# Two heads on the partition halves for the attention scores of a block-sparse attention and cos-MLP kernel on Trainium2

## The chip, the core and the metric

The kernel runs on one core of one Trainium2 chip. The metric is the time of one execution on the device in microseconds (us), as the median of several runs. The core has five engines that work side by side, each through its own list of instructions in a fixed order: TensorE (PE in the profile: matmuls; its weight loads stand apart as PEld), VectorE (DVE), ScalarE (ACT), GpSimd (POOL) and SyncE (SP), which here issues nearly all DMA transfers and does nothing else. Engines wait for each other by semaphores. TensorE and the others share no queue, but an instruction that waits holds back all that stand behind it in its own engine's list.

## What is computed

```python
def _attn_ref(q, k, v, sampled_blocks):           # 4 batches, 8 heads, 768 rows, 64 columns, fp32
    scores = np.matmul(q, k.transpose(0, 1, 3, 2)) / np.sqrt(D)
    mask = np.abs(blk_i - blk_j) <= 1              # blocks of 32 rows: 24 of them
    mask = mask | (blk_i == 0) | (blk_j == 0) | (blk_i == n_blocks - 1) | (blk_j == n_blocks - 1)
    for qb in range(n_blocks):
        for kb in sampled_blocks[qb]:              # three random blocks of keys for each block of queries
            mask[qb * block:(qb + 1) * block, kb * block:(kb + 1) * block] = True
    scores = np.where(mask, scores, -1000000000.0)
    attn = softmax(scores)
    return np.matmul(attn, v)

def _moe_ref(x, w_in, w_out):                      # x: 3072 x 512, w_in: 512 x 2048, w_out: 2048 x 512
    h = x @ w_in
    return (h * np.cos(h)) @ w_out
```

The output of the attention, laid out as 3072 rows of 512, is the x of the second function. All inputs are fp32.

## The kernel before

**Numbers.** Every fp32 operand of a matmul is split into two fp16 parts, a scaled high part and a low part (what the high part leaves). A product then takes several fp16 matmuls that add up in one PSUM bank: for the values and the MLP the terms high·high, high·low and low·high, for the scores all four.

**Tiles.** Queries are taken in 24 tiles of 128 rows, six for each batch. Five of them are sparse: each of a tile's four query blocks sees 11 blocks of keys, which are 352 columns, 256 of them common to the tile and 96 gathered for the block. The sixth is dense: the first and last block of the batch, which see all 768 keys, and the last 64 rows between. A unit of a sparse tile is a pair of heads (four units), one of a dense tile is one head (eight units). Two tiles make one step of the MLP, 256 rows (12 steps).

**A unit of attention.** `sparse_scores` (L1519) or `dense_scores` (L1545) write the scores of two heads, or of one head's two halves of keys, into the two banks of `sp`, of which there is one. `add_max` (L1558) adds the mask bias on VectorE, writes the result to `P` (four buffers) and keeps the row's maximum; `neg_max` (L1574) makes the bias of the exponent, `exp` (L1582) runs on ScalarE, `p_hi` and `p_lo` split the result into `ring` (three buffers), `p_transpose` (L1613) has a DMA transpose it into `PT` (three buffers), and `sparse_values` or `dense_values` multiply it with `V` into `xp`. `normalize` and `x_transpose` (L1678) turn a finished tile into its half of `xT`, from which `feed_forward` reads (L1828 up, L1878 down, which are matmuls of 256 and of 512 columns).

**The scores before.** Keys lie in `W` with the high part of one head in rows 0 to 63 and its low part in rows 64 to 127. Queries lie in `U` (two buffers) in two copies, one with high over low and one with low over high. Each copy times `W` is a matmul with all 128 rows, which makes two of the four terms at once. In a sparse unit each head and copy has one matmul of 192 columns (L1530), one of 64 (L1531), and four small ones of 96 columns (L1536) whose outputs are 32 rows each, which lie beside each other on the array (`tile_position=(0, 32 * j)`). This is `sparse_scores`:

```python
for z in range(2):
    u = U[:, z, h, :]
    mm(spv[:, :, 0:96], u, keys[:, :, 64 * i : 64 * i + 96], start=(z == 0), stop=False)
    mm(spv[:, :, 96:128]..., u, ends, start=False, stop=False)
```

**The copies of the queries.** For a tile after the fourth, `u_transpose` (L1457) has a DMA transpose the split queries from the buffer `n` into the first copy, and `u_swap` (L1462, L1464) has two more DMAs of 64 rows, which wait for the first, write the second copy from it. For the first four tiles `u_flip` (L1472, L1476) does both with TensorE, in two rounds with an eviction each by `u_put` (L1376, the shared `copy`).

**What sets the order.** `plan_kernel` (L522) makes all steps of all engines with an engine, a cost in us and a position; the position is a nominal one plus offsets from two tables, `PARAMS` and, by name, `NUDGES`. `Plan.run` (L397) then runs a list schedule over them: it takes the step that can start first by a simple model of the costs and, among those close to it, the one with the lowest position. It also hands out buffers, in the order of positions. The result is one fixed list for each engine; on the chip every engine follows its list and waits where the model was wrong.

Of the kernel before, what the change touches and what calls it, by code (L numbers as in the profile page):

```python
# [11 lines left out]
BF16 = mybir.dt.bfloat16  # L12
# [8 lines left out]
P = 128  # L21
# [35 lines left out]
NUDGES = dict(  # L57
    idx=-32.59, regs=19.28, regs0=-1.07, regs0_0=-2.88, regs1=6.62, regs1_0=10.29, regs2=1.07, regs2_0=-31.56, regs0_1=12.92, const=-2.31,
    kload=-0.13, kload0=-30.46, kload0_0=-8.81, ksq=11.63, ksq0=-3.65, ksq0_0=-30.09, ksq0_1=-32.78, kload0_2=-49.17, ksq0_2=1.23, kred=16.57,
    kred0=-13.01, kall=1.85, kall0=-40.47, ksc=-3.94, ksc0=-9.83, regs3=24.18, regs3_0=17.71, regs4=10.59, regs4_0=31.84, regs2_1=15.93,  # L60
    regs3_1=4.55, regs4_1=12.48, vload=2.48, vload0=-13.26, vload0_0=22.33, vsq=-5.99, vsq0=10.15, vsq0_0=50.09, vload0_1=0.11, vsq0_1=3.22,
    vload0_2=35.38, vsq0_2=9.63, vred=33.96, vred0=-15.73, vall=-0.58, vall0=2.01, vsc=-8.12, vsc0=2.74, ql=-1.06, ql0=8.22, qsq0=8.45, qsc=-7.13,
    qsc0=-6.37, qu=-1.96, qu0=-0.02, qnu=-18.18, qnu0=-9.18, qhi=-0.93, qhi0=-10.88, qlo=-5.87, qlo0=-9.35, uT=-0.55, uT0=-4.6, up=-0.48, up0=-6.98,
    khi=7.77, khi0=14.43, klo=15.69, klo0=21.95, kT=-0.02, kT0=6.82, kT0_2=1.62, kp=12.59, kp0=-20.67, kp0_2=2.03, kT0_3=0.47, kp0_3=-1.32,
    kT0_4=24.6, kp0_4=0.92, kT0_5=2.53, kp0_5=14.95, vhi=1.54, vhi0=14.31, vhi0_0=-0.32, vlo=5.56, vlo0=-1.09, vlo0_0=16.98, vst=7.46, vst0=36.73,
    vst0_0=3.28, vhi0_1=-5.72, vlo0_1=-16.01, vst0_1=28.16, vhi0_2=-26.22, vlo0_2=-5.63, vst0_2=12.95, vhi0_3=15.2, vlo0_3=0.02, vst0_3=27.76,
    vhi0_4=3.17, vlo0_4=3.32, vst0_4=-20.04, vhi0_5=27.65, vlo0_5=0.16, vst0_5=-21.14, vg=3.73, vg0_0=1.06, vg0_1=8.15, vg0_2=-14.78, vi=-7.5,
    vi0=6.3, vi0_0=-2.36, vi0_1=-12.83, vi0_3=13.91, wgd=-2.2, wgd0=-12.59, wga=0.68, wga0=20.44, wl=-4.41, wl0=-1.67, wc=-1.12, wc0=-0.25,
    wc0_0=0.05, wc0_1=-14.61, wsq=-3.18, wsq0=-2.46, wl1=-0.33, wc1=6.19, wc1_0=0.22, wc1_1=-3.2, wc1_2=3.2, wsq1=5.1, wl2=-26.1, wl3=-3.84,
    wc3_0=-0.59, wc3_1=-0.14, wc3_2=-6.37, wsq3=-2.11, wred=-0.94, wred0=-3.35, wall=1.38, wall0=23.2, wsc=-13.63, wsc0=-2.06, whi=0.24, whi0=13.15,  # L70
    wsi=-0.66, wsi0=-4.4, wlm=2.01, wlm0=-1.65, wlp=0.08, wlp0=-6.52, wlm1=0.71, wlp1=-7.37, whi2=-18.32, wlm2=1.35, wlp2=-0.9, wlm3=0.12,
    wlp3=-0.69, wl4=-7.09, wl5=-6.48, wc5=-5.38, wc5_0=15.11, wc5_1=-21.89, wc5_2=-1.33, wsq5=10, wl6=0.91, wl7=-14.86, wc7_1=25.08, wc7_2=12.48,
    wsq7=-30.63, wred4=17.52, wall4=2.06, wsc4=14.76, whi4=-4.06, wsi4=-2.52, wlm4=-4.15, wlp4=1, wlp5=5.53, whi6=-1.48, wlm6=-11.21, wlp6=6.93,
    wlp7=-6.67, wl8=-12.18, wl9=2.08, wc9=-7.98, wc9_0=-46.39, wc9_1=-4.24, wc9_2=-2.56, wsq9=-16.66, wl10=-1.79, wl11=17.97, wc11=-11.77,
    wc11_0=-2.11, wc11_1=-2.56, wc11_2=8.32, wsq11=-9.29, wsc8=2.64, whi8=32.97, wsi8=1.58, wlp8=-19.15, wlp9=-10.75, whi10=-17.36, wlm10=0.43,
    wlp10=-1.39, wlm11=4.47, wlp11=19.28, wl12=0.19, wl13=-22.97, wc13=14.49, wc13_0=-3.33, wc13_1=1.32, wc13_2=-12.78, wsq13=0.05, wl14=-1.87,
    wc14=-6.2, wc14_0=-7.86, wc14_1=-29.23, wc14_2=-4.96, wl15=31.58, wc15=-1.92, wc15_0=-3.83, wc15_1=20.07, wc15_2=-7.97, wsq15=1.03, wred12=6.05,
    wall12=9.18, wsc12=6.51, whi12=-11.82, wsi12=-6.71, wlm12=-1.47, wlp12=-0.2, wlm13=-2.27, wlp13=-5.13, whi14=-0.55, wlm14=-0.53, wlp14=1.2,
    wlm15=1.5, wlp15=-8.08, wl17=21.8, wc17=0.4, wc17_0=-16.55, wc17_1=-2.31, wc17_2=-2.05, wsq17=9.14, wl18=-1.04, wc18=-13.01, wc18_0=-2.02,
    wc18_1=3.07, wc18_2=-0.49, wsq18=6.03, wl19=-5.87, wc19=-0.16, wc19_0=8.28, wc19_1=-2.96, wc19_2=-5.86, wsq19=5.44, wred16=3.84, wall16=7.65,  # L80
    wsc16=-0.99, wlo=1.65, wlo16=-18.71, whi18=23.86, wlo18=2.49, wl20=3.86, wl21=-31.15, wc21=3.34, wc21_0=-3.38, wc21_1=-8.22, wc21_2=-20.01,
# [1875 lines left out]
```

## Time and profile before

| | |
|---|---|
| median of 3 runs | 894.15 us (890.65 to 894.72) |
| span of the profiled execution | 858.9 us |
| own time of the profiled execution | not recorded apart from its span; median less span is 35.25 us |
| TensorE busy in the span | 745.0 us, 87% |
| VectorE busy | 636.3 us, 74% |
| ScalarE busy | 640.3 us, 75% |

The span runs from the first to the last instruction of the profiled execution; the time of a run also holds what lies around it. Busy times are sums of an engine's instructions, so an engine at 87% was idle or waiting in the other 13%. The profile puts a wait down to what came last. "SPq" is the queue of SyncE, that is, the issue of a transfer; "DMA" is the transfer itself.

### The profile page before, as it was taken

What the parts mean: (1) busy time and instruction counts of PE and PEld (TensorE: products, weight loads), DVE (VectorE), ACT (ScalarE), POOL (GpSimd) and SP (SyncE); (2) the same over time, 40 slices, a digit from 0 to 9 for tenths busy, and PEclk for the clock granted to TensorE, in tenths of its full rate; (3) what the DMA queues carried; (4) which work ended last, traced back from release to release, by engine and by line L of the source; (5) the groups of instructions that cost most, each with busy time, mean ns of one, the idle gap of its engine ahead of it and who ended that gap; (6) DMA issues with size and microseconds to landing.
All of it is one profiled execution on the core that took longest, in us unless ns stands there. A gap on an engine that the chain in (4) does not pass through costs nothing.

```text
span 858.9 us, 23175 instructions
## 1 busy us (share of the span) xinstructions
PE 745.0 (87%) x9320; PEld 513.9 (60%) x9320; DVE 636.3 (74%) x1624; ACT 640.3 (75%) x1220; POOL 98.5 (11%) x128
## 2 busy tenths in 40 slices
PE   2575875888999988989999998999999879999997
PEld 2444563454757646847766557767675558576583
DVE  3987979898877775876857886968769756867361
ACT  1686956998868996896857988688769757869351
POOL 5212110000040012200030030200030112000000
PEclk9975896998999997999999998999999879999999
DMA  9999983669997998998895999896977995955300
GB/s 251 328 234 193 265 255 86 111 161 161 197 233 126 190 183 180 170 183 141 208 206 115 215 209 195 167 197 117 219 166 126 180 208 126 204 88 117 87 1 26
DMA packets 313308, 146.57 MB, mean 171 GB/s; under 512 B 266224, under 2 KB 290928, under 8 KB 313200
## 3 DMA queue, kind: packets, MB, share of 16 engines
q1 hardware_dynamic: 308080, 129.35, 73.4%
q0 software_dynamic: 5120, 15.73, 7.5%
q8 instruction: 73, 1.20, 0.6%
q14 instruction: 35, 0.29, 0.1%
HBM read 68.23 MB, written 12.58 MB: 94 GB/s over the span
## 4 chain that ended last, share of the span: by engine, by line
PE 51%; DMA 19%; DVE 15%; ACT 8%; issue 4%; SPq 2%; POOL 0%; DVEq 0%; ACTq 0%
PE ph L1828 19%; PE po L1878 19%; DMA PT<-ring 8%; DMA stage<-in_k_dram 3%; PE xp L1636 3%; DMA xT<-n 2%; PE sp L1530 2%; PE sp L1547 2%; DVE P L1563 2%; DVE ring L1599 2%; PE xp L1624 2%; PE sp L1536 2%; ACT P L1585 1%; DVE n L1287 1%; DVE g L1869 1%
## 5 line engine op out<-in xcount | busy, mean ns | idle before, releaser
L1828 PE MATMUL ph<-xT,w 128*128 128x256 f16 x2304 | 268.1, 276 | 8.6 <-DMA xT<-n 4.8
L1878 PE MATMUL po<-w,g 128*128 128x512 f16 x1152 | 269.2, 382 | 5.1 <-ACT g L1866 1.5
L1828 PEld LDWEIGHTS <-w 128*128 128x128 f16 x2304 | 225.7, 99 | 45.1 <-issue 4.3
L1878 PEld LDWEIGHTS <-g 128*128 128x128 f16 x1152 | 108.3, 98 | 125.1 <-issue 6.6
L1585 ACT ACTIVATE P<-P,sm 128x352 f32<-128x352 f32 (+1 forms) x224 | 151.9, 680 | 18.6 <-DVE sm L1578 9.4
L1502 POOL DMA_INDIRECT V<-scr,gidx x80 | 85.8, 1073 | 625.9 <-PE xp L1624 317.3
L1599 DVE TENSOR_TENSOR ring<-P,ring 128x704 f16<-128x704 f32 (+1 forms) x112 | 99.5, 906 | 37.1 <-ACT ring L1595 37.1
L1595 ACT CAST ring<-P 128x704 f16<-128x704 f32 (+1 forms) x112 | 86.0, 786 | 14.8 <-DMA PT<-ring 14.5
L1837 ACT ACTIVATE hs<-ph,sm 128x512 f32<-128x512 f32 x96 | 64.0, 679 | 44.0 <-PE ph L1828 39.6
L1563 DVE CUSTOM_DVE_ANT_1 P<-sp,bias 128x352 f32<-128x352 f32 x160 | 78.4, 518 | 23.3 <-PE sp L1536 22.6
L1530 PE MATMUL sp<-W,U 128*128 128x192 f16 x320 | 52.6, 265 | 21.0 <-DVE sm L1563 17.5
L1860 DVE SCALAR_TENSOR_TENSOR hs<-hs,sm,g 128x1024 f32<-128x1024 f32 x48 | 61.2, 1282 | 12.8 <-ACT g L1855 12.3
L1855 ACT ACTIVATE g<-g,sm 128x1024 f32<-128x1024 f32 x48 | 54.8, 1146 | 16.6 <-DVE g L1851 16.1
L1869 DVE TENSOR_TENSOR g<-hs,g 128x1024 f16<-128x1024 f32 x48 | 58.5, 1221 | 10.2 <-ACT g L1866 10.2
L1866 ACT ACTIVATE g<-hs 128x1024 f16<-128x1024 f32 x48 | 50.3, 1050 | 12.2 <-DVE hs L1860 11.9
L1851 DVE SCALAR_TENSOR_TENSOR g<-g,hs 128x1024 f32<-128x1024 f32 x48 | 58.5, 1221 | 0.8
L1847 DVE TENSOR_SCALAR g<-hs 128x1024 f32<-128x1024 f32 x48 | 32.9, 690 | 30.5 <-ACT hs L1837 29.0
L1624 PE MATMUL xp<-V,PT 96*32 96x64 f16 x1920 | 32.0, 205 | 24.0 <-DMA PT<-ring 20.9
L1531 PEld LDWEIGHTS <-U 128*128 128x128 f16 x320 | 33.0, 103 | 25.9 <-issue 22.2
L1531 PE MATMUL sp<-W,U 128*128 128x64 f16 x320 | 48.0, 205 | 0.0
L1636 PE MATMUL xp<-V,PT 128*128 128x64 f16 x960 | 47.2, 204 | 0.0
L1624 PEld LDWEIGHTS <-PT 96*32 96x32 f16 x1920 | 22.0, 103 | 39.7 <-DMA PT<-ring 26.8
(182 smaller groups left out, 939.3 us busy)
## 6 DMA issues: line engine op xcount, KB each, us to landing
V<-scr SPq DMA_DIRECT2D x20, 384.0 KB, 4.1
stage<-in_k_dram SPq DMA_DIRECT2D x12, 512.0 KB, 5.6
w<-in_moe_w_in_dram SPq DMA_DIRECT2D x12, 512.0 KB, 5.8
w<-in_moe_w_out_dram SPq DMA_DIRECT2D x12, 512.0 KB, 4.5
V<-scr SPq DMA_DIRECT2D x8, 768.0 KB, 5.2
scr<-n SPq DMA_DIRECT2D x21, 256.0 KB, 3.4
qs<-in_q_dram SPq DMA_DIRECT2D x20, 256.0 KB, 4.9
U<-U SPq DMA_DIRECT2D x40, 128.0 KB, 2.9
```

What stands on the lines that cost most here:

```text
L1502: self.nc.gpsimd.indirect_dma_start(V[:96, 2 + j, :], None, self.scr[b][:, :], bass.IndirectOffsetOnAxis(ap=self.gidx[:96, c : c + 1], axi ...
L1530: mm(spv[:, :, 0:96], u, keys[:, :, 64 * i : 64 * i + 96], start=(z == 0), stop=False)
L1531: mm(spv[:, :, 96:128].rearrange("p y (n c) -> p y n c", c=hf), u, ends, start=False, stop=False)
L1563: self.nc.vector.tensor_tensor_reduce(out=self.p_view(n, Pt)[:, a].rearrange("p (n c) -> p n c", c=hf), in0=sp[:, :w].rearrange("p (n c) - ...
L1585: self.nc.scalar.activation(Pv[:, a], Pv[:, a], AF.Exp, scale=qc[:, 4:5], bias=nb[:, bcol : bcol + 1], accum_out=sums[:, 2 * j + a : 2 * j ...
L1595: self.nc.scalar.copy(R[:, :, 0, : self.width(n)], self.p_view(n, Pt))
L1599: self.nc.vector.tensor_tensor(R[:, :, 1, :w], self.p_view(n, Pt), R[:, :, 0, :w], ALU.subtract)
L1624: mm(xp[32 * j : 32 * j + 32, h, :], PT[:96, 6 * a + 3 * l + 2, 32 * j : 32 * j + 32], V[:96, 2 + j, h, d0:d1], start=(a == 0 and x == 0), ...
L1636: mm(xp[:, h, :], PT[:, 6 * a + 3 * l + c, :], V[:, c, h, d0:d1], start=False, stop=(a == 1 and c == 1 and x == len(terms) - 1),)
L1828: self.nc.tensor.matmul(ph[:, ff, :], self.W1[p][:, wl, cc, c * P : (c + 1) * P], xT[:, xl * NCC + cc, :], start=(j == 0), stop=(j == len( ...
L1869: self.nc.vector.tensor_tensor(g[:, 1024:2048], hs, g[:, 0:1024], ALU.subtract)
L1878: self.nc.tensor.matmul(po, g[:, gl, ff, t * P : (t + 1) * P], self.W2[p][:, wl, ff, :], start=(first and ff == half * hf and j == 0), sto ...
```

## The change

The two heads of a pair now lie over each other: rows 0 to 63 of `W` hold one head and rows 64 to 127 the other, for the high parts in one place and for the low parts in another (`k_split`, `q_view`). A term of a score is then a matmul with 64 rows for each head, at row 0 or row 64 of the array, and a head has three terms instead of four: low·low is left out. The second copy of the queries is not made: `u_swap` and `u_flip` are gone, `U` is half as large, and the first four tiles use one round of transposes and one eviction.

- A sparse unit goes from 8 large and 16 small matmuls to 12 and 24, each with 64 rows.
- A unit of a dense tile becomes a pair of heads with one half of the keys (still eight units in a tile): 6 matmuls of 384 columns in place of 4. Both halves must be there before `neg_max` and `exp`, so `neg_max` runs once for every two units, for two heads at a time.
- The planner takes the positions of all steps from a new table, `PLACES`, has other costs, and a simple model of DMA (`DMAS`, `DMA_AHEAD`). So the order of all engines is new.

PE's list grows from 18594 to 20514 rows, SP's falls from 403 to 360 (the 40 transfers from `U` to `U` are gone), DVE's falls from 1770 to 1747, and ACT's grows from 923 to 951, with 46 loads of a function table in place of 42.

```diff
-            for z in range(2):
-                u = U[:, z, h, :]
-                mm(spv[:, :, 0:96], u, keys[:, :, 64 * i : 64 * i + 96], start=(z == 0), stop=False)
-                mm(spv[:, :, 96:128].rearrange("p y (n c) -> p y n c", c=hf), u, ends, start=False, stop=False)
...
+    def pairs(self, unit, U, W):
+        f, x = divmod(unit, 2)
+        hi = 4 * f + x
+        for ul, wl in ((0, 0), (0, 1), (1, 0)):
+            yield ul == 0 and wl == 0, ul == 1, U[:, 4 * ul + unit, :], W[:, hi + 2 * wl]
...
+            for part in range(2):
+                for a in range(2):
+                    r = slice(a * D, a * D + D)
...
+                    mm(out, u[r], x, start=(first and not part), stop=False, tile_position=(a * D, 0))
+        for _, final, u, keys in self.pairs(unit, U, Wg):
+            for j in range(4):
+                for a in range(2):
...
+                        tile_position=(a * D, 32 * j),
...
+    def dense_scores(self, unit, c, U, sp2):
...
+                self.nc.tensor.matmul(
+                    sp2[:, a, :384], u[r], keys[r, 384 * c : 384 * c + 384], start=first, stop=final, tile_position=(a * D, 0)
+                )
...
-    def u_swap(self, U, k):
-        D = self.D
-        if k:
-            self.nc.sync.dma_start(U[D : 2 * D, 1], U[0:D, 0])
-        else:
-            self.nc.sync.dma_start(U[0:D, 1], U[D : 2 * D, 0])
...
-            nc.vector.tensor_tensor(mx[:, 2:3], mx[:, 0:1], mx[:, 1:2], ALU.max)
-            nc.vector.tensor_scalar(nb[:, 0:1], mx[:, 2:3], nu, LN_PSCALE, op0=ALU.mult, op1=ALU.add)
...
+            nc.vector.tensor_tensor(mx[:, 0:2], mx[:, 0:2], mx[:, 2:4], ALU.max)
+        nc.vector.tensor_scalar(nb, mx[:, 0:2], nu, LN_PSCALE, op0=ALU.mult, op1=ALU.add)
...
-    idx=-32.59, regs=19.28, regs0=-1.07, regs0_0=-2.88, regs1=6.62, regs1_0=10.29, regs2=1.07, regs2_0=-31.56, regs0_1=12.92, const=-2.31,
...
+        o.pos = self.places.get(name if n == 1 else f"{name}#{n}", pos)
```

Three places show what moves. In the rows a name like `U_95` is one buffer of a tile, and the sizes are partitions by elements.

**SP at the queries of the tenth tile (batch 1).** Before, `U_95` is that tile's buffer; `n_90` are its split queries, `PT` and `ring` belong to the units of the tile ahead of it, `V_106` and `qs_93` to tiles to come.

```order
L1614 DMA_TRANSPOSE PT_104<-ring_100 128x12x128
L1457 DMA_TRANSPOSE U_95<-n_90 128x8x128
L1679 DMA_TRANSPOSE xT_110<-n_91 128x8x128
L1496 DMA V_106<-scr_122 16x2048
L1424 DMA qs_93<-in_q_dram 128x8x64
L1464 DMA U_95<-U_95 64x1024
L1462 DMA U_95<-U_95 64x1024
L1614 DMA_TRANSPOSE PT_103<-ring_100 128x12x128
L1614 DMA_TRANSPOSE PT_105<-ring_101 128x12x128
L1614 DMA_TRANSPOSE PT_104<-ring_102 128x12x128
```

After, `U_94` from `n_91` is the tenth tile's, and `U_94` held the ninth tile's queries too; `U_95` from `n_92` is the eleventh's, issued ahead of it.

```order
L1704 DMA_TRANSPOSE PT_105<-ring_100 128x12x128
L1556 DMA_TRANSPOSE U_95<-n_92 128x8x128
L1771 DMA_TRANSPOSE xT_109<-n_90 128x8x128
L1704 DMA_TRANSPOSE PT_103<-ring_101 128x12x128
L1704 DMA_TRANSPOSE PT_104<-ring_102 128x12x128
L1556 DMA_TRANSPOSE U_94<-n_91 128x8x128
L1704 DMA_TRANSPOSE PT_105<-ring_100 128x12x128
L1704 DMA_TRANSPOSE PT_103<-ring_101 128x12x128
L1704 DMA_TRANSPOSE PT_104<-ring_102 128x12x128
```

The two transfers from `U` to `U` are gone from between the transposes of `ring`. The tenth tile's queries now go into the buffer that the tile before it uses, so that transfer cannot start until that tile's last score. The same holds for the tiles 13, 15, 18 and 21; before, the two buffers alternated from tile to tile but once (at the tile 19).

**DVE at the second unit of a dense tile.** Before, the unit is one head; L1563 is `add_max` with its accumulator row behind it, L1577 and L1578 are `neg_max`, L1599 is `p_lo`.

```order
L1563 ISA P_97,sm<-sp_114,dbias 128x384
L1563 ISA sm 128x1
L1599 TENSOR_TENSOR ring_100<-P_98,ring_100 128x2x384
L1577 TENSOR_TENSOR sm<-sm 128x1
L1578 TENSOR_SCALAR sm<-sm 128x1
L1563 ISA P_98,sm<-sp_114,dbias 128x384
```

After, L1654 is `add_max`, L1668 and L1669 are `neg_max`, L1689 is `p_lo`; `P_97` is the second half of the keys of the first pair of heads, whose first half, `P_96`, stands some 20 rows ahead. The list is shown from the second of the two `add_max` on.

```order
L1654 ISA P_97,sm<-sp_114,dbias 128x384
L1654 ISA sm 128x1
L1755 TENSOR_SCALAR sm<-sm 128x8
L1961 TENSOR_TENSOR g_86<-hs_83,g_86 128x1024
L1762 RECIPROCAL sm<-sm 128x8
L1668 TENSOR_TENSOR sm<-sm 128x2
L1669 TENSOR_SCALAR sm<-sm 128x2
L1986 SCALAR_TENSOR_TENSOR kn_88<-po_119,sm,kn_88 128x512
L1689 TENSOR_TENSOR ring_102<-P_99,ring_102 128x2x352
L1689 TENSOR_TENSOR ring_101<-P_98,ring_101 128x2x352
L1654 ISA P_99,sm<-sp_114,dbias 128x384
```

Before, `neg_max` came once for every head, that is, for every unit; now it comes after every second unit and covers two heads, so that the first half waits in its buffer until the second is there.

**SP at the start of the program.** Before, the first rows are the sampled blocks, three loads of keys, three of values, the first queries and the first weights.

```order
L1144 DMA V_106<-in_sampled_blocks_dram 128x144
L1329 DMA stage_79<-in_k_dram 128x8x128
L1329 DMA stage_80<-in_k_dram 128x8x128
L1329 DMA stage_81<-in_k_dram 128x8x128
L1329 DMA hs_82<-in_v_dram 128x8x128
L1329 DMA hs_83<-in_v_dram 128x8x128
L1329 DMA g_84<-in_v_dram 128x8x128
L1424 DMA qs_93<-in_q_dram 128x8x64
L1714 DMA w_3_71<-in_moe_w_in_dram 128x1024
```

After, a load of output weights stands ahead of the keys.

```order
L1241 DMA V_106<-in_sampled_blocks_dram 128x144
L1806 DMA g_84<-in_moe_w_out_dram 128x1024
L1426 DMA stage_79<-in_k_dram 128x8x128
L1426 DMA stage_80<-in_k_dram 128x8x128
L1426 DMA stage_81<-in_k_dram 128x8x128
L1426 DMA hs_82<-in_v_dram 128x8x128
L1806 DMA w_3_71<-in_moe_w_in_dram 128x1024
L1523 DMA qs_93<-in_q_dram 128x8x64
L1426 DMA hs_83<-in_v_dram 128x8x128
```

The load of 512 KB into `g_84` moved from behind the keys and values to the second place, and one load of input weights moved ahead of the first queries.

## Rows read from the trace of the kernel before

**Rows 1.** The head of the profile's page and its line of busy times.

```profile
span 858.9 us, 23175 instructions
...
PE 745.0 (87%) x9320; PEld 513.9 (60%) x9320; DVE 636.3 (74%) x1624; ACT 640.3 (75%) x1220; POOL 98.5 (11%) x128
```

**Rows 2.** The chain of work that ended last, followed back from the last instruction: shares of the span by engine.

```profile
PE 51%; DMA 19%; DVE 15%; ACT 8%; issue 4%; SPq 2%; POOL 0%; DVEq 0%; ACTq 0%
```

**Rows 3.** Busy time of each engine in two stretches of the span, and in 20 us near the start (the last three columns are the granted clock of TensorE as a part of full speed, the busy share of the DMA engines and GB/s).

```profile
0.00:200.00 200.00, 130.50 (x1792) 90.27 (x1793) 163.12 (x451) 143.64 (x276) 33.05 (x68) 0.85 0.83 207
200.00:859.00 659.00, 614.51 (x7530) 423.67 (x7528) 473.13 (x1174) 496.67 (x945) 65.45 (x60) 0.97 0.81 159
20.00:40.00 20.00, 10.52 (x120) 8.79 (x120) 18.91 (x48) 12.63 (x21) 3.29 (x3) 1.00 1.03 326
```

**Rows 4.** What TensorE waited for between 200 and 859 us (engine, line and what came last; us in total, times, longest us).

```profile
PE xp L1624 <- DMA PT<-ring: 13.6, 10, 3.5
...
PE ph L1828 <- DMA xT<-n: 4.8, 3, 2.2
PE xp L1650 <- DMA PT<-ring: 3.5, 3, 1.4
```

**Rows 5.** The same view for the whole span, the two lines of the scores.

```profile
PE sp L1530 <- DVE sm L1563: 17.5, 14, 3.0
...
PE sp L1547 <- DVE sm L1563: 6.1, 3, 2.7
```

**Rows 6.** The timeline of TensorE at one sparse unit between two rounds of down matmuls (start us, us, operation; the length is that of the record from its start to its modelled end, and neighbours overlap).

```profile
663.16 0.25 PE L1530 MATMUL sp<-W,U 128*128 128x192 f16 x1
663.25 0.19 PE L1531 MATMUL sp<-W,U 128*128 128x64 f16 x1
663.28 0.25 PE L1530 MATMUL sp<-W,U 128*128 128x192 f16 x1
...
663.58 0.19 PE L1531 MATMUL sp<-W,U 128*128 128x64 f16 x1
663.71 0.35 PE L1536 MATMUL sp<-Wg,U 128*32 128x96 f16 x16
663.99 1.25 PE L1878 MATMUL po<-w,g 128*128 128x512 f16 x5
```

**Rows 7.** The same view at the small matmuls of a sparse unit with values right behind them, and at one head of a dense tile.

```profile
179.61 0.35 PE L1536 MATMUL sp<-Wg,U 128*32 128x96 f16 x16
179.79 0.35 PE L1624 MATMUL xp<-V,PT 96*32 96x64 f16 x24
180.08 0.52 PE L1636 MATMUL xp<-V,PT 128*128 128x64 f16 x12
180.44 2.75 PE L1878 MATMUL po<-w,g 128*128 128x512 f16 x12
183.03 0.81 PE L1547 MATMUL sp<-W,U 128*128 128x384 f16 x4
183.68 0.59 PE L1878 MATMUL po<-w,g 128*128 128x512 f16 x2
```

**Rows 8.** The chain at the start of the program, its first long transfer (start us, us, what).

```profile
2.29 8.22 DMA stage<-in_k_dram
```

**Rows 9.** Groups of instructions by line and form (busy us, mean ns of one; then idle time ahead of them).

```profile
L1855 ACT ACT_TABLE_LOAD x21 | 26.9, 1283 | 0.4
...
L1578 DVE TENSOR_SCALAR sm<-sm 128x1 f32<-128x1 f32 x32 | 6.8, 214 | 1.1
...
L1577 DVE TENSOR_TENSOR sm<-sm 128x1 f32<-128x1 f32 x32 | 4.9, 154 | 0.3
...
L1376 DVE COPY U<-ph 128x1024 f16<-128x1024 f16 x6 | 4.1, 677 | 0.2 <-PE ph L1472 0.2
...
L1376 ACT COPY U<-ph 128x1024 f16<-128x1024 f16 x2 | 2.0, 1002 | 2.6 <-PE ph L1472 2.6
```

**Rows 10.** The chain in the stretch from 300 to 325 us (start us, us, what).

```profile
310.17 6.15 DMA U<-n
...
316.38 0.47 SPq L1464
...
316.90 3.37 DMA U<-U
...
320.41 0.24 PE sp L1530
```

**Rows 11.** The timeline of TensorE in the same stretch, with what it waited for in brackets.

```profile
320.41 0.24 PE L1530 MATMUL sp<-W,U 128*128 128x192 f16 x1 [0.60 <-DMA U<-U]
...
322.33 0.24 PE L1530 MATMUL sp<-W,U 128*128 128x192 f16 x1 [1.14 <-DVE sm L1563]
...
327.35 0.51 PE L1624 MATMUL xp<-V,PT 96*32 96x64 f16 x24 [2.74 <-DMA PT<-ring]
```

**Rows 12.** The transfers that write U (issue in ns as least/median/most, first and last start in us).

```profile
L1457 SPq DMA_TRANSPOSE U<-n x20: 1232/1317/2597, 115.7 to 734.9; - x20
L1464 SPq DMA_DIRECT2D U<-U x20: 467/487/1016, 120.0 to 742.4; - x20
L1462 SPq DMA_DIRECT2D U<-U x20: 467/588/991, 121.2 to 743.0; - x20
```

**Rows 13.** What SyncE's queue waited for (us in total, times, longest us).

```profile
SPq L1464 <- DMA U<-n: 15.9, 9, 3.5
```

More of the change, by code (lines that the diff above doesn't have):

```diff
@@ L468, in run @@
             if pick is None:
-                raise RuntimeError("no runnable step: " + " ".join(o.name for c in ready.values() for o in c))
+                free_now = lambda o: all(slot_time(v) is not None for v in o.acq)
+                o = min((o for o in ops if o.end is None and not o.wait and o.need and free_now(o)), key=lambda o: (o.turn, o.n))
+                for v in o.acq:
+                    q = queues[v.cls]
+                    if q[0] is not v:
+                        x = q[0].ops[0]
+                        if not x.need:
+                            ready[x.eng].remove(x)
+                        x.need += 1
+                        q.remove(v)
+                        q.appendleft(v)
+                        o.need -= 1
+                if not o.need:
+                    ready_now(o)
+                continue
             t, o = pick[0][0], pick[1]
@@ L515, in run @@
                 x.need -= 1
+                x.wait -= 1
                 if not x.need:
@@ new lines, in attend @@
+            col = 0 if sparse else j % 2 * 2
+            for a in range(2):
+                op("DVE", 0.444 + x, pos + at(0) + pr["MX"] + 0.01 * a, lambda a=a, c=col + a, sp=sp, Pt=Pt, mx=mx: e.add_max(n, a, c, sp.t[:, a], Pt.t, mx.t),
+                   r=[(sp, a), bias if sparse else dbias], w=[(Pt, a), (mx, col + a)], name=f"mx{n}_{j}_{a}")
+            row.append((j, pos, vpos, Pt, R, PT))
+            if not sparse and j % 2 == 0:
+                continue
+            op("DVE", 0.13 if sparse else 0.33, pos + at(1) + pr["NB"], lambda mx=mx, nb=nb: e.neg_max(n, qc.t, mx.t, nb.t), r=[mx, u], w=[nb, (mx, 0)], name=f"nb{n}_{j}")
@@ L804, in attend @@
+            for k in row:
+                after_max(*k, nb)
+            row = []
         rs, y = Val("rs"), Val("ot")
@@ L1545, in dense_scores @@
-    def dense_scores(self, h, c, U, sp):
-        for z in range(2):
-            self.nc.tensor.matmul(
-                sp[:, c, :384], U[:, z, h, :], self.W[:, h, 384 * c : 384 * c + 384], start=(z == 0), stop=(z == 1)
-            )
+                        stop=final,
+                        tile_position=(a * D, 32 * j),
+                    )
+    def dense_scores(self, unit, c, U, sp2):
+        D = self.D
+        for first, final, u, keys in self.pairs(unit, U, self.W):
+            for a in range(2):
+                r = slice(a * D, a * D + D)
+                self.nc.tensor.matmul(
+                    sp2[:, a, :384], u[r], keys[r, 384 * c : 384 * c + 384], start=first, stop=final, tile_position=(a * D, 0)
+                )
```

818 lines of the change are left out of this document (439 added, 379 removed).

## The prediction

> **What bounds the kernel now.** I read the head of the page first. The profiled execution has a span of 858.9 us [rows 1]; the median of the runs is 894.15 us, so 35.25 us lie around the span, and I take these as fixed. TensorE is busy for 745.0 us, VectorE and ScalarE for some 640 each [rows 1]. TensorE also has the largest part of the chain, 51%, against 19% for transfers, 15% for VectorE and 8% for ScalarE [rows 2]. Then the stretches: in the first 200 us TensorE works for 130.50 us and is idle for 69.5, in the remaining 659 it works for 614.51 and is idle for 44.5 [rows 3]. So there are two regimes. Up to 200 us the data have to arrive and be split, with VectorE at 163.12 of 200 us and the DMA engines busy for 0.83 of the time. After it TensorE is the bound, and what can be won there is its own work plus at most 44.5 us of waits. The list of waits names them: on transposed exponentials 13.6 us in 10 waits and 3.5 in 3, on xT 4.8 in 3 [rows 4], which makes 21.9 us for transposes; and a score waits for `add_max` to empty `sp`, 17.5 us in 14 waits and 6.1 in 3 over the whole span [rows 5], which makes 23.6 us in 17, or 1.4 each.
>
> **Term 1, sparse scores on TensorE.** The reader should see in the timeline that the first large matmul starts at 663.16, the second copy's at 663.28, the first small one at 663.71 and the next down matmul at 663.99 [rows 6]. Four rounds of 192 and 64 columns at 0.11 are 0.44; the last starts at 663.58 and needs 0.03; then 0.10 go by until the small matmuls, which is what changing from full outputs to outputs of 32 rows costs. The unit takes 0.83. Where values with 32-row outputs follow, 16 small matmuls take 179.61 to 179.79, so 0.18, 11.3 ns each; without that neighbour it is 0.28, so the way back costs 0.10 again [rows 6, 7]. The 24 small value matmuls take 0.29 with one such change, so 7.9 ns each [rows 7]. After the change a unit has three rounds, if the two heads' halves run at once: 0.33. It pays 0.10 to enter the 64-row layout, 0.10 to the small ones, 24 × 7.9 ns = 0.19 for these, and 0.10 to leave: 0.82 for 0.83. Over 80 units this is −0.8 us. From below: small matmuls that also overlap across the two halves, 0.14, make it −4.8. From above: 11.3 ns each make it 0.90 and +5.6, and halves that run one after the other 1.23 and +32. I take the middle since 7.9 is the row with the like number of small matmuls.
>
> The Trainium skill, page "TensorEngine Tiling (Array Packing)", section "Key Properties", says that changing the tiling mode drains TensorE. The 0.10 us steps of these rows agree. It speaks against the change, since one more change of layout for each unit eats the round that is saved; the sum above holds that already.
>
> **Term 2, dense scores.** One head takes 183.03 to 183.68, 0.65 for four matmuls of 384 columns [rows 7], 0.162 each. A unit now has three rounds, 0.49, and enters and leaves the layout: 0.69, +0.04 in 32 units, +1.3 us. Without the changes of layout, where two such units follow each other, 0.49 and −5; one half after the other, 1.17 and +16.6.
>
> **Term 3, the start.** Four of the six evictions on VectorE go, 0.677 each, while the two of 1.002 on ScalarE stay [rows 9]; some of the four stand in the chain. 16 transposes of half a head for each of the first four tiles go on TensorE, which is not the bound there [rows 3]. Against it 512 KB of output weights stand ahead of the keys, whose load is the first long step of the chain, 8.22 us [rows 8]; at 326 GB/s [rows 3] this is 1.6 us. About −2 and +2: 0, with 3 either way. Weight loads ahead of the stores of V could add up to 8 us (five more of 512 KB), if the values of batch 0 wait for them; I leave that to the range.
>
> **Term 4, queries come sooner, buffers go later.** From the issue of `U<-n` to the first score it is 310.17 to 320.41: 6.15 for the transpose, then 0.47 to issue and 3.37 to land the second copy [rows 10]. The last two go, 3.84. TensorE waited there for 0.60, then 1.14 at the next score and 2.74 for exponentials [rows 11], whose transposes start later by what the scores came late. I take −2.5, from 0 to −3.84: the 1.14 stays, it is `sp`. Against it, at the tiles 10, 15, 18 and 21 the order writes the new queries into the buffer of the tile just ahead, and adding up the durations along TensorE's list gives only 5.8 to 7.2 us of work between the last score on it and the first new one, where the transpose takes some 6.2. Thus 0 to 0.4 each on time, more where SP is late: +1, up to +6. Together −1.5.
>
> **Term 5, SP and the DMA engines.** 20 issues at a median of 0.487 and 20 at 0.588 us go [rows 12], 21.5 us of SP's time, and 15.9 us in nine waits for the first copy [rows 13], behind which the transposes of the exponentials stood in SP's list. 40 × 128 KB are 5.2 MB, 16 us at 326 GB/s. The waits of TensorE that this can shorten are the 21.9 us on transposes. I take a fifth, −4; the ends are 0 (SP had slack, VectorE was late) and −12 (half of them).
>
> **Term 6, scores back to back.** A score waits for `add_max` only where little other work stands between it and the one before. By TensorE's lists, pairs with less than 1.25 us of work between them fall from 9 to 5 after the first MLP step, at 1.4 each [rows 5] −5.6. But both heads' scores now end together, where before the first was ready earlier, by 0.09 in a sparse unit (half of the small matmuls) and by 0.33 in a dense one (half of 0.65), so `add_max` begins later; for the few that are left, +1. Together −4.6.
>
> **Term 7, the rest.** Four more table loads at 1.283 [rows 9] are 5.1 us on ScalarE, of which by its 8% of the chain +0.4 count. `neg_max` runs 16 times less, 16 × (0.154 + 0.214) = 5.9 us on VectorE [rows 9]; since it sits idle for a quarter of the span, I count nothing. The exponentials of a first half now wait for the second; `P` has four buffers and holds two for it, and values stand far enough behind. If that cover fails it is one `add_max` wait, 1.4 for each of 16 pairs, at worst +22; I put it at 0 as few dense scores wait now [rows 5].
>
> **Sum.** −0.8 + 1.3 + 0 − 1.5 − 4 − 4.6 + 0.4 = −9.2, so 894.15 − 9.2 = 885 us. The matmuls themselves hardly change; what is won is in waits and in the order.
>
> **Rivals.** *The relief is hidden* (chance 0.18): SP had slack, the transposes of the exponentials are late because of `p_lo`, and term 5 is 0 and term 6 only −1. Then −1.6, 892.5 us, no change. For it: a transfer is named last in a wait also where its start was late. *The scores hold `sp` longer* (0.13), the case on the other side: if the later end of the first head is paid at every unit, because `add_max` and the next score are in the path, it is 80 × 0.09 + 32 × 0.33 = +17.8 in place of −4.6; then +13.2, 907 us. It decides from about half of the units on: −4.6 without term 6, and 9.1 more to be slower by 4.5. Against it: only 17 of 112 units waited before [rows 5]. *The halves overlap in part* (0.07): four small matmuls of 96 columns take 45 ns where 96 columns at 0.11 for 256 are 41 [rows 6, 7], so outputs of 32 rows overlap at 91% of perfect; one after the other would be 50%; halfway is 70%: a sparse unit gets 0.14 longer, a dense one 0.21, +11.2 + 6.7, so −9.2 + 17.9 = +8.7, 903 us. *The change doesn't do what it says* (0.05): 64-row terms run one after the other, −9.2 + 32.8 + 15.3 = +38.9, 933 us. No row of this kernel shows two matmuls on different rows of the array at once, so it can't be excluded.
>
> The Trainium skill, page "TensorE: Matmul & The Clock Gate", in the part on packing, gives a measured 3.07 for four row tiles at once, 77% of perfect. By an estimate from that figure the rows' 0.33 and 0.49 would become 0.43 and 0.63, and the sum some 12 us higher: the third rival at a lower price, and no change in the time. No row of the kernel before shows it.
>
> **How the numbers follow.** My forecast, 885 us, has 0.57. A measurement of this kernel tells some 0.5%, 4.5 us, from no change: the forecast is faster, its range 866 to 889. Faster 0.57; same 0.18 (the relief is hidden); slower 0.13 + 0.07 + 0.05 = 0.25. For the range: all favourable ends at once, −4.8, −5, −3, −3.8, −12 and −8, would give 858, which is not likely; of the 27 us between that and the forecast I take two thirds, 866. Above it, the two rivals at 903 and 907 are taken in and the serial one is left out. 866 to 908.
>
> **What would show it.** In the new timeline a sparse unit should occupy about 0.82 from its first matmul to the next step, a dense unit 0.69; 1.2 for either says serial halves. `U<-U` should be gone and a new tile's first score should wait 0 to 1 us for `U<-n` at the tiles 10, 15, 18 and 21. Waits on `PT<-ring` after the first 200 us should fall from 17.1 by about 4, those of scores on `add_max` from 23.6 to about 19. TensorE's idle time in the first 200 us should stay near 69.5. I am wrong if the idle time of TensorE rises, in the start above all, or if its granted clock falls in stretches where it was whole, as more waits of a few us would lead it to.

## The result, and the profile after

The changed kernel ran in 870.39 us (median of 4 runs, 863.76 to 873.81), the kernel before beside it in 893.38 us. The ratio is 0.9707, with a 95% interval of 0.9645 to 0.9769: 23 us or 2.9% faster where 9.2 us or 1% was forecast.

The page of the changed kernel, its head, its line of busy times and the shares of its chain, which answer to [rows 1, 2]:

```profile
span 862.0 us, 25014 instructions
...
PE 747.8 (87%) x10280; PEld 490.2 (57%) x10280; DVE 628.4 (73%) x1588; ACT 644.2 (75%) x1224; POOL 95.8 (11%) x128
...
PE 50%; ACT 18%; DVE 14%; DMA 7%; issue 6%; another core or an unknown queue 3%; SPq 1%; DVEq 0%; ACTq 0%
```

By these lines nothing was won: its span is 862.0, that of the first trace was 858.9 [rows 1]. The execution profiled here took 863.76 us by its own time, so 1.76 us lie around the span, not 35. The first trace was of an execution that must have taken some 861 us, 33 less than the runs beside it, so the two pages may not be set against each other. The experiments show a likely reason: on one chip (number 6) the kernel before took 863.9 us, on two others 893.5 and 897.9. Which chip the first trace comes from is not on record; its span and TensorE's 745.0 us fit chip 6, where they are 864.6 and 745.0. What follows compares runs of one chip, or ratios to the kernel before on the same chip, and says so where it can't.

The timeline of TensorE in the changed kernel (after), at a sparse unit followed by MLP matmuls, at one followed by values, and at a dense unit; this answers to [rows 6, 7]:

```profile
654.83 0.32 PE L1624 MATMUL sp<-Wg,U 64*32 64x96 f16 x24
655.09 2.79 PE L1920 MATMUL ph<-xT,w 128*128 128x256 f16 x24
...
660.00 5.34 PE L1970 MATMUL po<-w,g 128*128 128x512 f16 x24
665.28 0.51 PE L1619 MATMUL sp<-W,U 64*128 64x192 f16 x12
665.72 0.32 PE L1624 MATMUL sp<-Wg,U 64*32 64x96 f16 x24
665.97 0.36 PE L1714 MATMUL xp<-V,PT 96*32 96x64 f16 x24
```

```profile
179.58 0.66 PE L1638 MATMUL sp<-W,U 64*128 64x384 f16 x6
180.17 2.76 PE L1970 MATMUL po<-w,g 128*128 128x512 f16 x12
```

In the sparse unit the 12 large matmuls and the change to the small ones take 665.28 to 665.72, which is 0.33 + 0.11: three rounds, so the two heads' halves run at once. The 24 small ones with the change behind them take 0.26 (654.83 to 655.09) or 0.25. To enter costs 0.10: the 24 down matmuls from 660.00 on start 0.216 apart, so the score could have started at 665.18 and starts at 665.28. The unit occupies 0.79 to 0.80, forecast 0.82. The dense unit takes 0.59 with its exit and 0.69 with 0.10 to enter, as forecast.

The forecast set 0.83 before for every sparse unit. Where values follow, [rows 6, 7] give only 0.73 (0.55 to the small matmuls and 0.18 for these), since there was no layout to change behind them. In TensorE's list before, 28 of the 80 sparse units stand so, and these got longer.

### The profile page after: what moved, and what is told of

Read it like the earlier page. It is cut to its first block, busy times and chain, and to the rows that moved or that the text cites. A ratio compares the mean times of both kernels' runs of the same rounds, so it can differ in the third digit from the quotient of the medians.

```text
span 862.0 us, 25014 instructions
## 1 busy us (share of the span) xinstructions
PE 747.8 (87%) x10280; PEld 490.2 (57%) x10280; DVE 628.4 (73%) x1588; ACT 644.2 (75%) x1224; POOL 95.8 (11%) x128
## 4 chain that ended last, share of the span: by engine, by line
PE 50%; ACT 18%; DVE 14%; DMA 7%; issue 6%; another core or an unknown queue 3%; SPq 1%; DVEq 0%; ACTq 0%
PE po L1970 20%; PE ph L1920 19%; ACT P L1675 5%; DVE P L1654 3%; PE sp L1619 2%; ACT ring L1685 2%; PE xp L1726 2%; DVE ring L1689 2%; PE xp L1714 2%; DMA xT<-n 2%; ACT junk L1367 2%; DMA PT<-ring 2%; PE xp L1742 1%; PE sp L1624 1%
## 5 line engine op out<-in xcount | busy, mean ns | idle before, releaser
L1920 PE MATMUL ph<-xT,w 128*128 128x256 f16 x2304 | 275.3, 276 | 15.9 <-ACT hs L1929 7.1
L1920 PEld LDWEIGHTS <-w 128*128 128x128 f16 x2304 | 222.4, 99 | 59.9 <-issue 23.6
L1581 POOL DMA_INDIRECT V<-scr,gidx x80 | 84.0, 1049 | 630.2 <-PE xp L1714 326.6
L1654 DVE CUSTOM_DVE_ANT_1 P<-sp,bias 128x352 f32<-128x352 f32 x160 | 78.8, 519 | 57.0 <-remote 30.9
L1689 DVE TENSOR_TENSOR ring<-P,ring 128x704 f16<-128x704 f32 (+1 forms) x112 | 100.1, 905 | 19.5 <-ACT ring L1685 16.6
L1619 PE MATMUL sp<-W,U 64*128 64x192 f16 x960 | 45.8, 232 | 33.1 <-DVE sm L1654 31.2
L1952 DVE SCALAR_TENSOR_TENSOR hs<-hs,sm,g 128x1024 f32<-128x1024 f32 x48 | 61.2, 1281 | 17.8 <-ACT g L1947 17.7
L1619 PEld LDWEIGHTS <-U 64*128 64x128 f16 x960 | 32.8, 100 | 54.7 <-issue 51.9
L1714 PE MATMUL xp<-V,PT 96*32 96x64 f16 x1920 | 34.1, 200 | 12.8 <-issue 9.3
L1726 PE MATMUL xp<-V,PT 128*128 128x64 f16 x960 | 45.1, 200 | 0.0
L1675 ACT ACTIVATION_READ_ACCUMULATOR P<-P,sm 128x1 f32 x224 | 42.1, 188 | 0.0
L1654 DVE CUSTOM_DVE_ANT_1 P<-sp,dbias 128x384 f32<-128x384 f32 x64 | 33.7, 552 | 9.9 <-PE sp L1638 8.9
```

What stands on the lines that cost most here:

```text
L1581: self.nc.gpsimd.indirect_dma_start(V[:96, 2 + j, :], None, self.scr[b][:, :], bass.IndirectOffsetOnAxis(ap=self.gidx[:96, c : c + 1], axi ...
L1619: mm(out, u[r], x, start=(first and not part), stop=False, tile_position=(a * D, 0))
L1654: self.nc.vector.tensor_tensor_reduce(out=self.p_view(n, Pt)[:, a].rearrange("p (n c) -> p n c", c=hf), in0=sp[:, :w].rearrange("p (n c) - ...
L1675: self.nc.scalar.activation(Pv[:, a], Pv[:, a], AF.Exp, scale=qc[:, 4:5], bias=nb[:, a : a + 1], accum_out=sums[:, x : x + 1],)
L1689: self.nc.vector.tensor_tensor(R[:, :, 1, :w], self.p_view(n, Pt), R[:, :, 0, :w], ALU.subtract)
L1726: mm(xp[:, h, :], PT[:, 6 * a + 3 * l + c, :], V[:, c, h, d0:d1], start=False, stop=(a == 1 and c == 1 and x == len(terms) - 1),)
```

## The experiments

The theory after the result was that the gain comes from the new order, in the first 200 us above all, which keeps VectorE fed. Against it stood the prediction's own account, that the relief of SyncE and the end of the waits for copies, which belong to the steps, carry half of it, and, for the later part, that values stand farther behind their transposes.

**Both kernels on one chip.** No edit.

> The kernel before, as it is, for a profile whose own time is known. If some 35 us lie around the span of every execution, as the prediction assumed, its own time stands 35 us above its span: 894 and 859. If the profile that the prediction was read from was of a quicker execution, the own time stands 2 us above the span as in the changed kernel (863.76 and 862.0): a span of some 891, and the 32 us more than in the first trace show as idle time of TensorE or as a lower granted clock.

> The changed kernel, as it is, on the same chip as its variants: 864 to 874 us, 0.96 to 0.98 of the kernel before. Its sparse unit 0.79 to 0.83 us on TensorE, its dense unit 0.69.

On chip 6 the kernel before took 863.34 us (span 864.6, own time of that execution 866.51), so 1.9 us lie around a span, and the other 33 fit the difference between two chips. Neither of the two cases that were expected came out, because this run was on the quick chip too. The changed kernel took 831.32, ratio 0.960 (0.9526 to 0.9673), the better edge of what was expected. The windows of the kernel before and of the changed one on that chip, by columns as in [rows 3]:

```profile
0.00:200.00 200.00, 130.23 (x1758) 89.78 (x1762) 161.90 (x447) 142.16 (x273) 33.07 (x68) 0.86 0.83 206
200.00:900.00 700.00, 614.74 (x7566) 423.14 (x7566) 474.54 (x1178) 498.14 (x949) 63.33 (x60) 0.97 0.78 151
```

```profile
0.00:200.00 200.00, 145.39 (x2200) 96.32 (x2201) 174.90 (x485) 158.93 (x309) 32.34 (x68) 0.85 0.91 222
200.00:900.00 700.00, 589.29 (x8082) 389.97 (x8080) 453.45 (x1104) 484.48 (x916) 64.34 (x60) 0.97 0.73 139
```

The idle time of TensorE in the first 200 us falls from 69.8 to 54.6, by 15.2. After them it falls from 49.9 to 41.3, by 8.5 (the stretch less the busy time, up to each span's end). Its busy time falls by 10.3. These are the 34.0 us between the spans. The trace's record of the granted clock splits the busy time: at the upper level (2.4 GHz) it is 656.3 us before and 658.4 after, at the lower (1.2 GHz) 88.7 and 76.3. So the whole fall lies in stretches at the lower level. If a microsecond there counts for half, which is an estimate, TensorE has 4 us less work and the clock gives the other 6. (The record begins at 40.4 us before and at 23.5 after. Ahead of it the page shows 1.00, as for 20 to 40 us in [rows 3], but 128 columns take 107 ns there, and 256 take 109 at the upper level, so this split counts that stretch as lower.) VectorE does 174.90 us of its work in the first 200 us, where it did 161.90.

**The new steps in the old order, and the old steps in the new order.** Both kernels make their lists by emitting steps in one global order. In these two the planner's order is replaced by a list of names taken from the other kernel; the step with the lowest place whose inputs and buffers are there comes next (`rank_of` gives a step's place in the other kernel's order).

```diff
-    pl.run(PARAMS["DELTA"], PARAMS["TSTICK"], PARAMS["MSTICK"])
+    replay(pl, rank_of())
```

> The changed kernel's steps (three terms, two heads on the halves, no copies of the queries), issued on all engines in the order of the kernel before as far as the data allow. If the gain of 23 us comes from the steps (transfers and waits for copies gone), this stands near the changed kernel: 870 to 876. If it comes from the new order, this stands near the kernel before: 888 to 895. If the forecast's split is right (about half each: terms 4 and 5 in the steps, term 6 in the order), 880 to 885.

> The kernel before with its own steps (four terms in two matmuls of 128 rows, the copies of the queries by two transfers three rows later in SyncE's list), issued on all engines in the order of the changed kernel. If the gain is in the steps: 888 to 900. If in the order: 868 to 876. Split in half: 878 to 886. The order was made for other steps, so it may also be slower than both, above 900, where queries wait for their copies behind the single buffer at the tiles 10, 13, 15, 18 and 21: 5 x 4 us.

Neither gains: 0.999 (0.9951 to 1.0029) and 1.009 (1.0041 to 1.0139), where both together give 0.960 on the same chip. TensorE's waits after 200 us, first of the kernel before, then with the new steps in the old order, then with the old steps in the new order, then of the changed kernel (us, times, longest); this answers to [rows 4]:

```profile
PE xp L1624 <- DMA PT<-ring: 18.9, 12, 4.1
PE sp L1530 <- DVE sm L1563: 9.3, 7, 3.0
...
PE xp L1650 <- DMA PT<-ring: 3.1, 5, 1.0
```

```profile
PE xp L1936 <- DMA PT<-ring: 13.5, 11, 4.0
PE sp L1841 <- DVE sm L1876: 13.0, 11, 3.1
PE xp L1964 <- DMA PT<-ring: 3.2, 2, 1.9
```

```profile
PE sp L1771 <- DMA U<-U: 19.0, 3, 8.8
...
PE xp L1865 <- DMA PT<-ring: 8.3, 6, 2.3
PE sp L1788 <- DMA U<-U: 6.2, 1, 6.2
```

```profile
PE xp L1714 <- DMA PT<-ring: 10.6, 8, 2.9
PE sp L1619 <- DVE sm L1654: 8.2, 7, 2.1
...
PE xp L1742 <- DMA PT<-ring: 2.0, 2, 1.7
...
PE sp L1619 <- DMA U<-n: 0.3, 1, 0.3
```

The windows of the two mixed kernels, the new steps in the old order first:

```profile
0.00:200.00 200.00, 129.68 (x2019) 85.16 (x2020) 162.27 (x446) 143.33 (x275) 33.82 (x68) 0.85 0.81 206
```

```profile
0.00:200.00 200.00, 143.12 (x1949) 100.19 (x1950) 170.10 (x472) 150.64 (x292) 33.60 (x68) 0.91 0.89 215
```

Read together: the new order alone brings TensorE's idle time in the first 200 us to 56.9 us, with the old steps too, and loses it later, where scores wait 25.2 us for copies. The new steps alone leave the start at 70.3; values wait 5.3 us less for their transposes (16.7 for 22.0) and scores 3.7 more for `add_max` (13.0 for 9.3). So neither the steps nor the order gain alone. The smaller idle time at the start comes with the order, whichever the steps. Later the new order needs the copies gone: between its two kernels lie 42 us (1.009 and 0.960), of which 25.2 are these four waits, near the 5 x 4 us that were expected. In the old order there was hardly such a wait to take away: TensorE's matmuls waited once for a copy, for 0.60 us, in the first trace [rows 11], and never in the one of chip 6. The other 17 us are not traced to a cause.

**New order first, and old order first.** The new steps, with the order changed over behind the last step of the weights' conversion. In short (the kernels hold the whole lists):

```python
order = NEW[:779] + [k for k in OLD if k not in NEW[:779]]      # the other kernel: OLD[:769], then NEW
```

> The changed kernel's steps in the new order up to the last piece of the weights' conversion (779 of 3126 steps, about the first 200 us), then in the old order. Theory A (the gain of the order lies in the start, where VectorE's list is kept fed: idle 2 instead of 12 us between 100 and 200): 0.975 to 0.982 of the kernel before, TensorE idle in the first 200 us some 55 us instead of 70, the rest as in the old order. Rival B (it lies in the steady part, where values stand farther behind their transposes): 0.995 to 1.00.

> The same steps, the old order for the first 769 (to the same piece of the weights), then the new one. Theory A: 0.98 to 0.99, the smaller part, some 10 us from waits after 200 us. Rival B: 0.965 to 0.975. If the two parts only work together, both mixtures stand above 0.985.

Ratios 0.9944 (0.9901 to 0.9987) and 1.0044 (1.0008 to 1.0079), on chip 1. The first stands at the edge of rival B's range and the second outside both theories; as a pair they fit the third case, that the parts work only together. Up to about 197 us every engine's list is that of the new order in the first mixture, and that of the old one in the second. The first mixture has TensorE idle for 65.6 us in the first 200 and 75 after them, the second 77.2 and 65, by the same reading of the windows as above (spans 896.5 and 898.3):

```profile
0.00:200.00 200.00, 134.41 (x2060) 88.89 (x2061) 160.39 (x446) 141.87 (x272) 35.54 (x68) 0.87 0.85 207
200.00:900.00 700.00, 621.51 (x8220) 406.47 (x8219) 468.19 (x1142) 500.65 (x950) 63.30 (x60) 0.95 0.71 143
```

```profile
0.00:200.00 200.00, 122.82 (x1879) 81.14 (x1880) 151.80 (x425) 134.30 (x258) 33.78 (x68) 0.76 0.78 200
200.00:900.00 700.00, 633.50 (x8403) 412.69 (x8401) 478.92 (x1164) 511.27 (x967) 62.57 (x60) 0.95 0.74 145
```

So on this one chip the new start does save TensorE 11.6 us of idle time, as theory A has it. Behind the seam both mixtures wait more than the changed kernel, which has 61.0 and 53.9 us of idle time on chip 3 (span 866.5):

```profile
0.00:200.00 200.00, 139.01 (x2084) 92.53 (x2084) 163.39 (x455) 146.17 (x282) 32.25 (x68) 0.86 0.86 210
200.00:900.00 700.00, 612.58 (x8198) 399.30 (x8196) 464.82 (x1136) 498.05 (x943) 61.74 (x60) 0.96 0.72 142
```

What is won ahead of the seam is lost behind it. Whether an order made for another state of the buffers can't keep it, or the seam itself is at fault, these runs don't show.

**Weights later, and weights earlier.** VectorE's conversions of the weights are a third of its work in the start: the front calls all inputs fp32, but the weights arrive in fp64, and the three lines that convert them hold VectorE for 52.5 us of the first 200 before and for 52.2 after. The waits of VectorE and of SyncE's queue in the kernel before, between 100 and 200 us on chip 6:

```profile
DVE xT L1722 <- DMA w<-in_moe_w_out_dram: 2.9, 1, 2.9
```

```profile
SPq L1424 <- DVE sm L1279: 17.4, 1, 17.4
SPq L1457 <- PE po L1788: 9.8, 1, 9.8
```

A conversion waits for its load, and the loads stand behind steps for which SyncE waits 17.4 and 9.8 us. Hence two kernels that move the weight loads in SyncE's list. In short:

```python
ORDER = move_loads(NEW, OLD)    # late: the k-th weight load ahead of the SyncE step that follows OLD's k-th
ORDER = move_loads(OLD, NEW)    # early: the same the other way round
```

> The changed kernel in its own order on every engine but SyncE, where the k-th of the 32 weight loads is issued where the old order issues its k-th; nothing else in SyncE's list moves. Theory A with its cause (weights are issued ahead of keys and values, so VectorE's conversions never wait): 0.97 to 0.985, VectorE waits 5 to 15 us more for weights before 200 us. Rival (the place of the loads does not matter, the order of VectorE and ScalarE does): 0.958 to 0.965, as the changed kernel.

> The changed kernel's steps in the old order, with only the 32 weight loads moved in SyncE's list to where the new order has its k-th. If the early loads alone feed VectorE in the first 200 us: 0.982 to 0.988 of the kernel before (15 us less than the 0.999 of the same order without the move), VectorE busy 95 or more between 100 and 200 us. If the order of VectorE's and ScalarE's own lists does it: 0.993 to 1.003.

Late loads cost far more than either theory said: 1.0337 (1.0265 to 1.0408). VectorE waits 35.3 us for weights in the first 200, where 5 to 15 were expected:

```profile
DVE w L2021 <- DMA w<-in_moe_w_out_dram: 14.3, 4, 6.5
DVE w L2021 <- DMA w<-in_moe_w_in_dram: 11.6, 2, 8.6
DVE stage L2021 <- DMA w<-in_moe_w_in_dram: 9.4, 2, 7.1
```

But more than the loads moved here. A conversion is not emitted ahead of its load, so 195 of the 1588 VectorE instructions in the trace stand elsewhere than in the changed kernel, with 146 of TensorE's and 71 of ScalarE's. Early loads left the other lists as they were, but for five of VectorE's rows. In the old order they gain nothing: 1.017 (1.0116 to 1.0223). How much they lose isn't shown, as the same order without the move, 0.999, ran on another chip. The windows of the two kernels at the start, late loads first:

```profile
0.00:200.00 200.00, 93.94 (x1409) 63.24 (x1410) 115.26 (x331) 93.49 (x188) 33.64 (x68) 0.74 0.65 170
```

```profile
0.00:200.00 200.00, 116.81 (x1843) 79.39 (x1844) 142.87 (x401) 124.77 (x241) 33.59 (x68) 0.84 0.74 192
```

VectorE gets 115.26 and 142.87 us of work done in the first 200, where the changed kernel gets 163.39 on chip 3. That chip is also the one of the early loads; the late ones ran on chip 1. So loads in places that were made for other lists cost time, and the theory that early loads alone feed VectorE falls.

**The copies put back, read and unread.** For the tiles from the fifth on, two transfers of 128 KB follow the queries' transpose three rows later in SyncE's list.

```diff
+    def u_copy(self, U, k):
+        D = self.D
+        self.nc.sync.dma_start(U[k * D : k * D + D, 1], U[k * D : k * D + D, 0])
...
-            yield ul == 0 and wl == 0, ul == 1, U[:, 4 * ul + unit, :], W[:, hi + 2 * wl]
+            yield ul == 0 and wl == 0, ul == 1, U[:, copied if ul else 0, 4 * ul + unit, :], W[:, hi + 2 * wl]
```

> The changed kernel with the two transfers of 128 KB put back for the tiles from the fifth on: they copy the queries within their rows, three rows later in SyncE's list, and the third term reads the copy, so scores wait for it. All else is the new order. By the forecast's terms 4 and 5 undone (+1.5 + 4): 0.965 to 0.97. By the wait for copies in the old steps under the new order (25.7 us in 5 waits): 0.985 to 0.995.

> The changed kernel, as it is, beside the three variants that follow: 0.96 to 0.971 of the kernel before.

> The changed kernel with the two transfers of 128 KB put back three rows behind the queries' transpose, but read by no matmul: SyncE waits, the DMA engines and the buffer of the queries have their load, no score waits for a copy. By the forecast's term 5 (the traffic and SyncE's time are worth 4 us): +4 us, 0.5% above the changed kernel. If only the wait of the scores counts (11.7 us were seen with the copies read): 0 to +2 us.

Read, the copies give 0.9866 (0.9794 to 0.9939) on chip 1; unread 0.9712 (0.9666 to 0.9759) on chip 3, where the changed kernel itself gives 0.9728 (0.9684 to 0.9773). So the transfers and SyncE's time cost nothing that can be told: 4 us more than the changed kernel would be 872.8 us, and the four runs lie between 865.98 and 870.11. The wait costs some 12 us (0.9866 against 0.9728 is 1.4%). That is rough: the two intervals leave 5 to 20 us, and no run of the changed kernel was on chip 1. TensorE's waits with the copies read:

```profile
PE sp L1627 <- DMA U<-U: 7.7, 6, 3.6
...
PE sp L1646 <- DMA U<-U: 4.0, 2, 3.8
```

They are 11.7 us in 8 waits, about as much. But TensorE's idle time in the whole span is only 8.0 us above that of the changed kernel on chip 3 (122.9 and 114.9) and its busy time 8.8 above (760.4 and 751.6), at a mean granted clock of 0.926 for 0.937. How much of that is the chip's is not shown.

**Four terms.** Low times low put back.

```diff
-        for ul, wl in ((0, 0), (0, 1), (1, 0)):
-            yield ul == 0 and wl == 0, ul == 1, U[:, 4 * ul + unit, :], W[:, hi + 2 * wl]
+        for ul, wl in ((0, 0), (0, 1), (1, 0), (1, 1)):
+            yield ul == 0 and wl == 0, ul == 1 and wl == 1, U[:, 4 * ul + unit, :], W[:, hi + 2 * wl]
```

> The changed kernel with low times low put back as a fourth term of 64 rows for each head: four large rounds for three and 32 small matmuls for 24 in a sparse unit, 8 for 6 in a dense one. If TensorE bounds: 80 x (0.11 + 0.05) + 32 x 0.16 = +18 us, 2.1% above the changed kernel, and a sparse unit of 0.95 us, a dense one of 0.85. If the scores stand in the shadow of waits: below +8 us.

The ratio is 0.9836 (0.9758 to 0.9915): 883.77 us (875.0 to 889.5) against 868.81 for the changed kernel on the same chip, +15. The busy lines of the changed kernel and of the one with four terms on chip 3, and a sparse unit of the latter:

```profile
PE 751.6 (87%) x10280; PEld 491.8 (57%) x10280; DVE 628.2 (72%) x1588; ACT 644.2 (74%) x1224; POOL 94.0 (11%) x128
```

```profile
PE 769.4 (87%) x11304; PEld 509.3 (58%) x11304; DVE 627.4 (71%) x1588; ACT 644.5 (73%) x1224; POOL 95.5 (11%) x128
```

```profile
661.59 0.62 PE L1619 MATMUL sp<-W,U 64*128 64x192 f16 x16
662.14 0.36 PE L1624 MATMUL sp<-Wg,U 64*32 64x96 f16 x32
662.43 2.76 PE L1970 MATMUL po<-w,g 128*128 128x512 f16 x12
```

The unit takes 0.84 from its first matmul and 0.94 with its entry, 0.15 more than with three terms. TensorE's busy time grows by 17.8 us, and about 15 of it arrive at the end: the added matmuls do not hide in waits. Put the other way, leaving low times low out is worth some 15 of the 25 us by which the changed kernel beats the one before on this chip.

## Why the prediction came out as it did

The direction and the range were right. As the prediction had it, the kernel became faster through waits and the order and hardly through the matmuls, whose third term only pays for the changes of layout: on chip 6, 23.7 of the 34.0 us are idle time of TensorE, and the rest is busy time at the lower clock. The size was 2.5 times too small, and the terms that carried the forecast are not those that carried the result. That the range held is in part luck: its lower end was made mostly of the favourable ends of terms 5 and 6, which gave nothing.

- **What the sum started from** was wrong: the 35.25 us around the span don't exist, and the trace was of a quicker execution than the runs. The terms weren't touched by that; their ratio, 0.990, is what to compare with 0.9707 on the first chip, 0.960 on chip 6 and 0.9728 on chip 3.
- **Terms 1 and 2** hold: 0.79 to 0.80 for a sparse unit where 0.82 was forecast, 0.69 for a dense one. The price before, 0.83 for all 80 units, overlooked the 28 with values behind them, at 0.73. By these figures term 1 comes to about −0.4 us (an estimate: 52 times −0.04 and 28 times +0.06), not −0.8. The rivals of halves that run one after the other, or overlap in part, fall by the timeline.
- **Term 3 is the one that was mis-sized.** It was set to 0 with 3 either way, from single evictions and one load, and it measured −15.2 us of TensorE's idle time on chip 6, nearly half of the gain there. I had pointed at VectorE in the first 200 us, with 163.12 of 200 us [rows 3], but priced only the work that went and not the 37 us in which it waited; the new lists let it do 13.0 us more in the same time. This comes with the order: the old steps in it have 56.9 us of idle time there, for 69.8 before and 54.6 after. That the loads of weights do this by themselves was my theory after the result, and it fell.
- **Term 4** priced a wait that exists, of scores for copies, but hardly in the order that it was read from. It rested on the one wait of [rows 11]; the old order hid the other copies, and the new steps, which need none, gain nothing there that can be told (0.999). In the new order, read copies cost some 12 us. The price of a buffer used twice in a row, set to +1 at four tiles (by the front there is a fifth, 13), was 0.3 us in one wait of TensorE; it went to SyncE's queue, where the queries' transpose waits for scores:

```profile
SPq L1556 <- PE sp L1624: 11.9, 4, 4.6
```

- **Term 5 fell.** The relief of SyncE and of the DMA engines was to give 4 us; with the transfers put back unread the time is the same within the intervals. Waits on transposed exponentials did fall after 200 us, from 22.0 to 12.6, more than the 4 foreseen. The new steps alone have 16.7 and the new order alone 9.4, where waits for copies may hide some; so steps and order both bear on it, and the waits don't tell how much each is worth in time.
- **Term 6 fell.** Scores waited 24.1 us for `add_max` on chip 6 before (18.0 in 14 waits and 6.1 in 3, over the whole span) and 23.5 after (21.2 in 17 and 2.3 in 4), where 4.6 less was forecast: by the lists fewer scores stand back to back, but there are 21 such waits for 17. The counterpart, that both heads end together, may be what shows in the old order as 3.7 us more after 200 us, where I had +1; no run takes it apart. The rival on the other side, which has this at every unit, would then have had a fifth of its price. The waits before and after, on chip 6:

```profile
PE sp L1530 <- DVE sm L1563: 18.0, 14, 3.0
...
PE sp L1547 <- DVE sm L1563: 6.1, 3, 2.7
```

```profile
PE sp L1619 <- DVE sm L1654: 21.2, 17, 2.5
...
PE sp L1638 <- DVE sm L1654: 2.3, 4, 1.3
```

- **The rival of the hidden relief** had terms 5 and 6 nearly right, 0 and −1 for 0 and −0.6 measured. Its time, 892.5, was wrong all the same, since it left term 3 at 0 too.
- **Term 7** was not tried by itself. No row of the runs speaks against it.

What stays open: which steps of the new order keep VectorE busy at the start, as the loads alone don't; why the two halves of that order don't add up; and what the changed kernel takes on chip 1, against which the price of the read copies would have to be set.

## What to carry to other kernels

Price an edit and the order that it allows apart: taking the copies away was worth nothing in the old order, which hid them, and some 12 us in the new one, which doesn't. In a stretch that another engine limits, add up that engine's idle time, not only the work removed from it; that is the most that a new order can win there, and here it won 13 of 38 us. And before reading a trace against a time, look whether the time belongs to that execution: a gap of 35 us between a span and a median is a question, not a constant.

## What the runs showed of the hardware

- The same program takes 3.4 to 4.5% longer on some chips: the kernel before 863.9, 893.5 and 897.9 us on chips 6, 3 and 1, the changed one 831.3 and 868.8 on chips 6 and 3. The mean granted clock was the same, 0.937, in the two profiled executions of the changed kernel. No run shows the cause.
- Matmuls of 64 rows at row 0 and row 64 of the array run fully at once: a pair of 192 and 64 columns takes 0.11 us for two heads (0.55 with four rounds, 0.44 with three), what one of 128 rows takes for one.
- Eight places of 64 rows by 32 columns overlap too: 24 matmuls of 96 columns take 0.26 us with the change of layout behind them, so 6.7 ns each if that change is the 0.10 us of the other rows. Eight more of them add 0.03 to 0.04, so 4 to 5 ns each; either is below the 11.3 ns of the 128-row ones [rows 7].
